# A fused mLSTM and MoE kernel: column sums in column groups, a turned branch, and attention steps moved in two chunks

## Chip, cores, metric

One core of one Trainium2 chip. The metric is the device time of one execution in microseconds (us). Runs are compared in the same state: for one core, a run that lies over 1.5% above the fastest of its kernel counts as slow and is left out of ratios. A ratio is the mean time of one kernel's fast runs over the mean of the other's fast runs of the same rounds, so it is not quite the ratio of the medians quoted beside it.

In profile lines PE is TensorE, PEld its weight loads, ACT ScalarE, DVE VectorE, POOL GpSimd and SP SyncE; a q behind a name is that engine's instruction queue. `a<-b` names an output and its inputs, and a bracket at the end of a line is the idle time before it and what ended it. PSUM is the memory that matrix products are written to; `hp` is the tile there that holds the product with w_in. The tail is the time from the start of the last VectorE output operation to the end of the span.

## The reference

Two stages, the second on the result of the first, in float32 at the outside:

```
q, k, v, o_gate: [4, 8, 768, 40]   i_gate, f_gate: [4, 8, 768]
for t in range(768):                      # per batch and head: a matrix memory C, a vector n
    C = f_stab * C + i_stab * outer(v[t], k[t]);   n = f_stab * n + i_stab * k[t]
    y[t] = sigmoid(o_gate[t]) * (C @ q[t]) / max(|n . q[t]|, 1)
x = y as [3072, 320]                      # tokens x (heads * head_dim)
g = s * relu(x @ w_in) ** 2 + b           # w_in: [320, 2048]
out = g @ w_out                           # w_out: [2048, 320]
```

The kernel uses that b adds the same row to every token: `out = s * (relu(..)**2 @ w_out) + b * colsum(w_out)`. The column sums of w_out, spread over 128 partitions and times b, are the tile `brep`.

## The kernel before

Tokens are handled in six chunks of 512. While the matrix products of chunk c run (16 steps of about 1.28 us), the attention of chunk c+1 is put between them at fixed steps by `put(chunk, step, ...)`. A general block for other gate values stands behind a branch at the end and is jumped over. Parts (cuts marked):

```python
self.psH = ctx.enter_context(tc.tile_pool(name="psH", bufs=2, space=PSUM))   # the two hp buffers
...
def load_x(self, bb, eng, names="qo"):          # 640 KB of q, then 640 KB of o_gate
    ...
    eng.dma_start(out=self.x32[nm, bb, 0], in_=src)

def relu(self, c, k, a):                        # ScalarE; frees an hp buffer
    self.nc.scalar.activation(out=r1, in_=self.hp.pop((c, k, a)), func=ACT.Relu)

def bias(self, f0, f1):                         # column sums, spread, with a matrix of ones
    ...
    for f in range(f0, f1):
        nc.tensor.matmul(ps[:], lhsT=self.ones[:], rhs=self.wo[:, f, :], start=(f == 0), stop=(f == NF - 1))
    if f1 == NF:
        nc.vector.tensor_scalar_mul(out=self.brep, in0=ps, scalar1=self.bc[:, 0:1])

def events(self):
    ...
    put(0, 15, self.bias, 0, 8)
    put(1, 0, self.vw, 2, a.copy)               # cast of v, batch 2, on ScalarE
    put(0, 15, self.kw, 2)                      # kp = k * weights, batch 2, on VectorE
    put(1, 1, self.bias, 8, NF)
    ... 2: (1, 2, 4, 6, 8, 1, 2, 6, 9, 11),     # chunk 2: q0, r0, t0, h0, y0, q1, r1, t1, h1, y1
        # q: cast q on ScalarE   r: transposing DMA on SP   t: tanh   h: ps_h   y: transposing DMA of x
    put(1, 2, self.ev_cn, 2)                    # needs v and kp of batch 2
    put(1, 3, self.load_x, 3, self.nc.sync)     # chunk 3's q and o_gate, on SP

def run(self):
    ...
    for k in range(4):
        if c > 0:
            self.mm1_rem(c, k, 0)               # 2 matmuls of 64 rows, into one hp buffer each
            self.mm1_rem(c, k, 1)
        for a in range(2):
            self.mm1(c, k, a)                   # 4 whole matmuls into hp
            self.square(*prev); self.relu(c, k, a)
            ...                                 # two steps of events, each with mm2 of chunk c-1

with tc.If(short.asked > 0, preferred_fallthrough_block=False), ExitStack() as inner:
    Full(inner, tc, short).run()
```

Of the kernel before, what the change touches and what calls it, by code (L numbers as in the profile page):

```python
# [8 lines left out]
F32 = mybir.dt.float32  # L9
# [22 lines left out]
class Short:  # L32
# [50 lines left out]
    def load_rest(self):  # L83
        nc, d = self.nc, self.d
        nc.gpsimd.dma_start(out=self.sc, in_=d["s"].partition_broadcast(P))
        nc.gpsimd.dma_start(out=self.bc, in_=d["b"].partition_broadcast(P))
        self.load_kv(2, B, nc.gpsimd)

    def load_rest2(self, eng):
        d = self.d  # L90
# [72 lines left out]
    def masks_late(self):  # L163
        nc, c = self.nc, self.const
        self.tri42 = c.tile([P, P], BF16, name="tri42")
        nc.gpsimd.memset(self.tri42, 1.0)
        nc.gpsimd.affine_select(
            out=self.tri42, in_=self.tri42, pattern=[[1, P]], base=0, channel_multiplier=-1,
            compare_op=ALU.is_ge, fill=0.0,
        )  # L170
        self.sel = c.tile([P, 3, L], BF16, name="sel")
        nc.gpsimd.tensor_copy(out=self.sel, in_=self.idb[:, 0:L].unsqueeze(1).to_broadcast([P, 3, L]))
        nc.gpsimd.memset(self.ib2[:, :, 1:2], 2.0)

    def gates(self):

# [145 lines left out]
    def ev_h(self, c, i, early=False):  # L322
        nc = self.nc
        bb, _ = self.pair(c, i)
        pool, tag = (self.psH, "hp") if early else (self.psB, "b")
        ps = pool.tile([P, 2, 512], F32, tag=tag, name="ps_h")
        qt = self.qt.pop((c, i))
        for j in range(2):
            for g in range(3):
                w = 123 if g < 2 else 82  # L330
                if c >= B and j == 0:
                    lhs, rhs = self.pm[bb][:, g, :], self.vbd[bb]
                else:
                    lhs, rhs = qt[0 : 3 * D, j, g, :], self.cn[bb]
                nc.tensor.matmul(  # L335
                    ps[:, j, g * 123 : g * 123 + w], lhsT=lhs,
                    rhs=rhs[:, g, :, :].rearrange("k a e -> k (a e)")[:, 0:w], start=True, stop=True,
                )
        hv = ps[:, :, 0 : H * (D + 1)].rearrange("p j (h e) -> p j h e", h=H)

        d1 = self.work.tile([P, 2, H], F32, tag="d1", name="d1")
        if c >= B:
            nc.vector.scalar_tensor_tensor(
                out=d1, in0=hv[:, :, :, D], scalar=-2.0,
                in1=self.ib2[:, bb * H : (bb + 1) * H, :].rearrange("p h j -> p j h"), op0=ALU.mult, op1=ALU.max,
            )
        else:
            nc.vector.tensor_scalar(  # L348
                out=d1, in0=hv[:, :, :, D], scalar1=-2.0, scalar2=2.0, op0=ALU.mult, op1=ALU.max
            )  # L350
        dd = self.work.tile([P, 2, H], F32, tag="dd", name="dd")
        nc.vector.scalar_tensor_tensor(
            out=dd, in0=hv[:, :, :, D], scalar=2.0, in1=d1, op0=ALU.mult, op1=ALU.max
        )
        rec = self.work.tile([P, 2, H], F32, tag="rec", name="rec")
        nc.vector.reciprocal(
            out=rec[:, :, :].rearrange("p j h -> p (j h)"), in_=dd[:, :, :].rearrange("p j h -> p (j h)")
        )
        fac = self.work.tile([P, 2, H, D], F32, tag="fac", bufs=2, name="fac")
        x = self.x[c, i] = self.work.tile([P, 2, DM + 64], BF16, tag="x", name="x")  # L360
        th = self.th.pop((c, i))
        for j in (slice(0, 1), slice(1, 2)) if early else (slice(0, 2),):
            nc.vector.tensor_tensor(  # L363
                out=fac[:, j, :, :], in0=hv[:, j, :, 0:D],
                in1=rec[:, j, :].unsqueeze(3).to_broadcast([P, j.stop - j.start, H, D]), op=ALU.mult,
            )
            nc.vector.scalar_tensor_tensor(  # L367
                out=x[:, j, 0:DM], in0=th[:, j, :, :].rearrange("p j h d -> p j (h d)"), scalar=1.0,
                in1=fac[:, j, :, :].rearrange("p j h d -> p j (h d)"), op0=ALU.add, op1=ALU.mult,
            )  # L370
            nc.vector.tensor_copy(out=x[:, j, DM:], in_=x[:, j, 2 * P : DM])

    def ev_x(self, c, i, js=(0, 1)):
        nc = self.nc
        x = self.x[c, i]
        ps = self.psO.tile([P, 2, 3, P], BF16, tag=self.spare, name="ps_x")
        for kts in ((0, 1), (2,)):
            for j in js:
                for kt in kts:
                    nc.tensor.transpose(ps[:, j, kt, :], x[:, j, kt * P : (kt + 1) * P], self.idb[:])  # L380
        t0 = self.pair(c, i)[1]
        nc.scalar.copy(out=self.xt[:, t0 + js[0] : t0 + js[-1] + 1, :, :], in_=ps[:, js[0] : js[-1] + 1, :, :])  # L382

# [52 lines left out]
        f = 4 * k + a  # L436
        self.nc.vector.tensor_tensor(out=self.g[c][:, f : f + 3 : 2, :], in0=r1, in1=r1, op=ALU.mult)  # L437

    def bias(self, f0, f1):
        nc = self.nc  # L440
        if f0 == 0:
            self.ps_b = self.psB.tile([P, DM], F32, tag="b", name="ps_b")
        ps = self.ps_b
        for f in range(f0, f1):
            nc.tensor.matmul(ps[:], lhsT=self.ones[:], rhs=self.wo[:, f, :], start=(f == 0), stop=(f == NF - 1))  # L445
        if f1 == NF:
            self.brep = self.keep.tile([P, DM], F32, name="brep")
            nc.vector.tensor_scalar_mul(out=self.brep, in0=ps, scalar1=self.bc[:, 0:1])

    def mm2(self, c, tb, f0, f1, pool=None):  # L450
        nc = self.nc
        if f0 == 0:
            if pool is None:
                self.o2[c, tb] = self.psO.tile([P, DM], F32, tag=f"o{tb % 2}", name="o2")
            else:
                self.o2[c, tb] = self.psH.tile([P, DM], F32, tag="hp", name="o2t")
        for f in range(f0, f1):
            nc.tensor.matmul(  # L458
                self.o2[c, tb][:], lhsT=self.g[c][:, f, tb * P : (tb + 1) * P], rhs=self.wo[:, f, :],
                start=(f == 0), stop=(f == NF - 1),  # L460
            )
        if f1 == NF:
            osb = self.work.tile([P, DM], F32, tag="osb", bufs=5, name="osb")
            nc.vector.scalar_tensor_tensor(  # L464
                out=osb, in0=self.o2.pop((c, tb)), scalar=self.sc[:, 0:1], in1=self.brep, op0=ALU.mult, op1=ALU.add
            )
            out = self.d["out"]
            if c < B:
                r0 = c * S + P
                dst = out[r0 : r0 + N, :].rearrange("(p j) n -> p j n", j=CT)[:, tb, :]  # L470
            else:
                i, j = divmod(tb, 2)
                r0 = self.pair(c, i)[0] * S + 5 * P * j
                dst = out[r0 : r0 + P, :]
            eng = nc.gpsimd if c < 3 else nc.sync
            eng.dma_start(out=dst, in_=osb)  # L476



# [46 lines left out]
    def events(self):  # L526
# [10 lines left out]
        put(0, 3, self.ev_q, 1, 0, v)  # L537
        put(0, 3, self.ev_q, 1, 1, v, True)
        put(0, 5, self.tanh, 1, 0)
        put(0, 6, self.ev_h, 1, 0)  # L540
        put(0, 6, self.square, 0, 0, 1)
        put(0, 7, self.tanh, 1, 1)
        put(0, 10, self.ev_x, 1, 0)
        put(0, 10, self.ev_h, 1, 1)
        for n in range(2, 8):
            put(0, 9 + min(n, 6), self.square, 0, n // 2, n % 2)
        put(0, 15, self.ev_x, 1, 1)
        put(0, 15, self.bias, 0, 8)
        put(1, 0, self.vw, 2, a.copy)
        put(0, 15, self.kw, 2)  # L550
        put(1, 10, self.vw, 3, a.copy)
        put(1, 1, self.bias, 8, NF)
        for c in range(2, 6):
            d = c - 1

            q0, r0, t0, h0, y0, q1, r1, t1, h1, y1 = {
                2: (1, 2, 4, 6, 8, 1, 2, 6, 9, 11),
                3: (-7, -6, 0, 1, 4, -6, -4, 2, 5, 8),
            }.get(c, (-11, -10, 0, 1, 4, -10, -9, 2, 5, 8))
            for at, step in (  # L560
# [12 lines left out]
            if c >= B:  # L573
                put(d - 1, 14, self.ev_s, c, 0)
                put(d, 3, self.ev_s, c, 1)
        put(1, 2, self.ev_cn, 2)
        put(1, 12, self.kw, 3)
        put(1, 14, self.ev_cn, 3)
        put(2, 8, self.make_tri)
        for c, b0 in ((2, 0), (3, 2)):  # L580
# [1 line left out]
            put(c, 11, self.ev_vr, b0)  # L582
            put(c, 12, self.ev_kt, b0 + 1)
            put(c, 15, self.ev_vr, b0 + 1)
        put(1, 3, self.load_x, 3, self.nc.sync)
        put(1, 14, self.load_rest2, self.nc.sync)
        put(1, 14, self.load_y, 0, self.nc.sync)
        put(2, 10, self.load_y, 2, self.nc.sync)
# [7 lines left out]
    def start(self):  # L596
# [12 lines left out]
        self.masks_late()  # L609
        for k in range(4):  # L610
            self.load_wo(k)
        self.load_x(2, nc.gpsimd)
        self.ps_w = self.psO.tile([P, 512], F32, tag="o0", name="ps_w")
        self.warm(34)
# [22 lines left out]
    def run(self):  # L637
        nc, tc = self.nc, self.tc
        with tc.manual_schedule():
# [3 lines left out]
            for c in range(6):  # L643
                for k in range(4):
# [4 lines left out]
                    elif k == 0:  # L649
# [3 lines left out]
                            self.mm1(0, 0, a, 0, N // 2)  # L653
                            self.ev_x(0, 1, (a,))
                        self.ev_cn(1)
                        self.warm(8)
                    for a in range(2):
                        if c == 0:
                            n0 = N // 2 if k == 0 else 0
# [185 lines left out]
def kernel(  # L845
# [16 lines left out]
    with ExitStack() as inner:  # L862
        short.pools(inner)
        short.run()
    with tc.If(short.asked > 0, preferred_fallthrough_block=False), ExitStack() as inner:
        Full(inner, tc, short).run()


# [28 lines left out]
```

## Time and profile before

| | before |
|---|---|
| time, median of 3 runs | 142.49 us (142.13 to 142.72) |
| span of the profiled run | 140.5 us |
| TensorE (PE) busy | 133.6 us, 95% |
| chunk 1's first whole matmuls (L423) begin | 29.67 us |
| chunk 2 begins (64-row matmuls, L411 x4) | 49.55 us |
| last VectorE output operation to end of span | 4.86 us |

### The profile page before, as it was taken

To read this page: it belongs to the slowest core of one execution; us is meant where nothing else is said; L and a number is where in the kernel's file an instruction comes from. 1 tells how busy PE (TensorE), PEld (TensorE's weight loads), DVE (VectorE), ACT (ScalarE), POOL (GpSimd) and SP (SyncE) were. 2 spreads that over 40 slices of the span, in tenths; PEclk is the share of its full clock that TensorE was granted. 3 is DMA by queue.
4 is the path that set the end of the run, shared out by engine and by line. 5 is a ranking of instruction groups with operands and counts; after the bars stand their busy time and mean duration, and the time that the engine had idled before them with its cause. 6 is when DMAs were issued, how large, how long until landed. Compare 5 with 4: busy or idle time off the path is not lost.

```text
span 140.5 us, 2582 instructions
## 1 busy us (share of the span) xinstructions
PE 133.6 (95%) x979; PEld 78.2 (56%) x979; DVE 91.5 (65%) x201; ACT 69.9 (50%) x91; POOL 26.8 (19%) x58
## 2 busy tenths in 40 slices
PE   6998999999999999999999999999999999999960
PEld 7985643446555655565565465555545545557730
DVE  6679748895499759776769956688962635335130
ACT  3273479758559545943366653383435443550000
POOL 6889399100101110011011011100000000000000
PEclk9999999999999999999999999999999999999998
DMA  3999969994899899999983471017221110011211
GB/s 41 316 217 272 283 121 122 191 314 132 176 324 178 171 200 212 210 155 148 215 127 61 103 159 47 0 47 88 66 58 47 47 51 18 34 49 49 96 51 56
DMA packets 42412, 18.45 MB, mean 131 GB/s; under 512 B 31840, under 2 KB 41376, under 8 KB 42392
## 3 DMA queue, kind: packets, MB, share of 16 engines
q1 hardware_dynamic: 36412, 10.67, 38.2%
q0 software_dynamic: 5280, 7.43, 23.8%
q10 hardware_dynamic: 700, 0.11, 0.5%
q8 instruction: 9, 0.15, 0.5%
q14 instruction: 11, 0.09, 0.2%
HBM read 13.75 MB, written 3.93 MB: 126 GB/s over the span
## 4 chain that ended last, share of the span: by engine, by line
PE 76%; DVE 0%; issue 0%
PE o L458 31%; PE hp L423 26%; PE hp L411 8%; PE o2t L458 6%; PE ps_h L335 2%; PE ps_b L445 1%; PE ps_vr L256 1%; PE ps_s L313 0%; PE ps_kt L241 0%; DVE osb L464 0%; PE ps_cn L226 0%; PE ps_fl L502 0%; PE ps_fm L509 0%; PE ps_tri L204 0%
## 5 line engine op out<-in xcount | busy, mean ns | idle before, releaser
L430 ACT ACTIVATE r<-hp 128x1024 bf16<-128x1024 f32 x48 | 49.0, 1024 | 47.6 <-PE hp L423 44.4
L458 PE MATMUL o<-wo,g 128*128 128x320 bf16 x320 | 52.7, 299 | 0.0
L423 PE MATMUL hp<-xt,wi 128*128 128x512 bf16 (+1 forms) x200 | 49.9, 372 | 0.0
L458 PEld LDWEIGHTS <-g 128*128 128x128 bf16 x384 | 36.4, 98 | 17.8
L437 DVE TENSOR_TENSOR g<-r 128x1024 bf16<-128x1024 bf16 x48 | 32.5, 685 | 9.9 <-ACT r L430 9.7
L423 PEld LDWEIGHTS <-wi 128*128 128x128 bf16 x200 | 17.1, 97 | 22.6 <-issue 9.4
L476 POOL DMA_DIRECT2D out_dram<-osb x12 | 6.5, 544 | 59.4 <-DVE osb L464 59.4
L464 DVE SCALAR_TENSOR_TENSOR osb<-o,sc,brep 128x320 f32<-128x320 f32 x20 | 10.9, 548 | 9.1 <-PE o L458 8.7
L411 PE MATMUL hp<-xt,wr 64*128 64x512 bf16 (+1 forms) x100 | 15.8, 373 | 0.4 <-ACT xt L382 0.2
L367 DVE SCALAR_TENSOR_TENSOR x<-th,fac 128x640 bf16<-128x640 f32 (+1 forms) x14 | 10.2, 730 | 1.3
L524 PE MATMUL ps_w<-ones 128*128 128x128 bf16 x106 | 9.7, 258 | 1.1 <-POOL ones L134 1.1
L363 DVE TENSOR_TENSOR fac<-ps_h,rec 128x640 f32<-128x640 f32 (+1 forms) x14 | 10.2, 728 | 0.4
L524 PEld LDWEIGHTS <-ones 128*128 128x128 bf16 x106 | 8.3, 118 | 1.1 <-POOL ones L134 1.1
L458 PE MATMUL o2t<-wo,g 128*128 128x320 bf16 x64 | 8.9, 299 | 0.0
L411 PEld LDWEIGHTS <-wr 64*128 64x128 bf16 x100 | 3.6, 94 | 8.0 <-issue 7.3
L464 DVE SCALAR_TENSOR_TENSOR osb<-o2t,sc,brep 128x320 f32<-128x320 f32 x4 | 2.2, 551 | 5.7 <-PE o2t L458 5.7
L292 ACT ACTIVATE th<-ox 128x640 f32<-128x640 f32 x8 | 5.7, 729 | 0.2 <-DMA ox<-in_o_gate_dram 0.2
L288 ACT CAST qb<-qx 128x160 bf16<-128x160 f32 (+1 forms) x11 | 4.2, 443 | 2.9 <-DMA qx<-in_q_dram 2.9
L335 PE MATMUL ps_h<-cn,qt 120*128 120x123 bf16 (+1 forms) x60 | 5.0, 212 | 0.0
L382 ACT COPY xt<-ps_x 128x384 bf16<-128x384 bf16 (+1 forms) x6 | 3.5, 584 | 3.0 <-PE ps_x L380 3.0
L335 PEld LDWEIGHTS <-qt 120*128 120x128 bf16 x60 | 3.8, 98 | 1.0 <-DVE qt L306 0.2
L348 DVE TENSOR_SCALAR d<-ps_h 128x16 f32<-128x16 f32 x8 | 1.4, 173 | 4.4 <-PE ps_h L335 4.4
(98 smaller groups left out, 87.6 us busy)
## 6 DMA issues: line engine op xcount, KB each, us to landing
out_dram<-osb POOLq DMA_DIRECT2D x12, 160.0 KB, 2.9
out_dram<-osb SPq DMA_DIRECT2D x12, 160.0 KB, 1.8
qx<-in_q_dram SPq DMA_DIRECT2D x2, 640.0 KB, 4.8
ox<-in_o_gate_dram SPq DMA_DIRECT2D x2, 640.0 KB, 6.7
qx<-in_q_dram POOLq DMA_DIRECT2D x2, 640.0 KB, 8.7
ox<-in_o_gate_dram POOLq DMA_DIRECT2D x2, 640.0 KB, 9.2
wo<-in_moe_w_out_dram POOLq DMA_DIRECT2D x4, 320.0 KB, 6.9
qy<-in_q_dram SPq DMA_DIRECT2D x8, 160.0 KB, 4.2
```

The costliest lines, as they stand in the source:

```text
L292: self.nc.scalar.activation(out=th, in_=self.src("o", c, i), func=ACT.Tanh, scale=0.5)
L335: nc.tensor.matmul(ps[:, j, g * 123 : g * 123 + w], lhsT=lhs, rhs=rhs[:, g, :, :].rearrange("k a e -> k (a e)")[:, 0:w], start=True, stop= ...
L363: nc.vector.tensor_tensor(out=fac[:, j, :, :], in0=hv[:, j, :, 0:D], in1=rec[:, j, :].unsqueeze(3).to_broadcast([P, j.stop - j.start, H, D ...
L367: nc.vector.scalar_tensor_tensor(out=x[:, j, 0:DM], in0=th[:, j, :, :].rearrange("p j h d -> p j (h d)"), scalar=1.0, in1=fac[:, j, :, :]. ...
L411: nc.tensor.matmul(hp[:, e, n0:n1], lhsT=self.wr[64 * e : 64 * e + 64, k, a * P : (a + 1) * P], rhs=self.xt[64 * e : 64 * e + 64, t0:t1, 2 ...
L423: nc.tensor.matmul(hp[:, e, n0:n1], lhsT=self.wi[:, kt, f * P : (f + 1) * P], rhs=self.xt[:, t0:t1, kt, :], start=False, stop=(kt == 1),)
L430: self.nc.scalar.activation(out=r1, in_=self.hp.pop((c, k, a)), func=ACT.Relu)
L437: self.nc.vector.tensor_tensor(out=self.g[c][:, f : f + 3 : 2, :], in0=r1, in1=r1, op=ALU.mult)
L458: nc.tensor.matmul(self.o2[c, tb][:], lhsT=self.g[c][:, f, tb * P : (tb + 1) * P], rhs=self.wo[:, f, :], start=(f == 0), stop=(f == NF - 1),)
L464: nc.vector.scalar_tensor_tensor(out=osb, in0=self.o2.pop((c, tb)), scalar=self.sc[:, 0:1], in1=self.brep, op0=ALU.mult, op1=ALU.add)
L476: eng.dma_start(out=dst, in_=osb)
L524: self.nc.tensor.matmul(self.ps_w[:, 0:P], lhsT=self.ones[:], rhs=self.ones[:], start=True, stop=True)
```

## The change

Intent: take PE work out of the bias (16 matmuls of the full array become 16 in four column groups of 32, which may run side by side, and three for the spread); shorten the start; let the branch be jumped over without a late jump; and move steps of chunks 0 and 1 to fit. `kv` of batch 2 is loaded between the parts of w_out. The core of the diff:

```diff
@@ load_rest / start
-        self.load_kv(2, B, nc.gpsimd)
             self.load_wo(k)
+            if k == 1:
+                self.load_kv(2, B, nc.gpsimd)
@@ masks_late: self.fours, zero but for rows 0, 32, 64, 96 (cut)
@@ ev_h / ev_x: chunks 0 and 1 do not copy x's last 64 columns, but transpose them twice
-            nc.vector.tensor_copy(out=x[:, j, DM:], in_=x[:, j, 2 * P : DM])
+            if c > 1:
+                nc.vector.tensor_copy(out=x[:, j, DM:], in_=x[:, j, 2 * P : DM])
+            for a in (0, 64):
+                nc.tensor.transpose(ps[a : a + 64, j, 2, :], x[:, j, 2 * P : DM], self.idb[:])
@@ bias(f0, f1) becomes
+    def colsum(self):
+        for f in range(NF):
+            j = 32 * (f % 4)
+            nc.tensor.matmul(
+                ps[j : j + 32, :], lhsT=self.ones[:, 0:32], rhs=self.wo[:, f, :], start=(f < 4), stop=(f >= NF - 4)
+            )
+        ... three bfloat16 parts ws0..2 of ps, five VectorE operations (cut)
+    def bias(self):
+        for i in range(3):
+            nc.tensor.matmul(ps[:], lhsT=self.fours[:], rhs=self.ws[i], start=(i == 0), stop=(i == 2))
+        nc.vector.tensor_scalar_mul(out=self.brep, in0=ps, scalar1=self.bc[:, 0:1])
@@ mm2: the output part becomes osb(c, tb); block (0, 0) is put out later, by an event
-        if f1 == NF:
+        if f1 == NF and (c, tb) != (0, 0):
+            self.osb(c, tb)
@@ events (squares, ev_h and ev_x of chunk 0 moved too, cut)
-        put(0, 15, self.bias, 0, 8)
-        put(0, 15, self.kw, 2)
-        put(1, 1, self.bias, 8, NF)
-        put(1, 2, self.ev_cn, 2)
+        put(1, 0, self.kw, 2)
         put(1, 0, self.vw, 2, a.copy)
+        put(1, 1, self.ev_cn, 2)
+        put(1, 3, self.colsum)
+        put(1, 6, self.bias)
+        put(1, 7, self.osb, 0, 0)
-                2: (1, 2, 4, 6, 8, 1, 2, 6, 9, 11),
+                2: (4, 5, 7, 8, 10, 4, 5, 9, 10, 12),
-        put(1, 3, self.load_x, 3, self.nc.sync)
+        put(1, 6, self.load_x, 3, self.nc.sync)
@@ run
-                        self.warm(8)
+                        self.warm(2)
-    with tc.If(short.asked > 0, preferred_fallthrough_block=False), ExitStack() as inner:
+    with tc.If(short.asked > 0, preferred_fallthrough_block=True), ExitStack() as inner:
```

More of the change, by code (lines that the diff above doesn't have):

```diff
@@ L173, in masks_late @@
         nc.gpsimd.memset(self.ib2[:, :, 1:2], 2.0)
+        self.fours = c.tile([P, P], BF16, name="fours")
+        nc.gpsimd.memset(self.fours, 0.0)
+        for j in range(0, P, 32):
+            nc.gpsimd.memset(self.fours[j : j + 1, :], 1.0)
     def gates(self):
@@ L376, in ev_x @@
         ps = self.psO.tile([P, 2, 3, P], BF16, tag=self.spare, name="ps_x")
-        for kts in ((0, 1), (2,)):
-            for j in js:
-                for kt in kts:
-                    nc.tensor.transpose(ps[:, j, kt, :], x[:, j, kt * P : (kt + 1) * P], self.idb[:])
+        for j in js:
+            for kt in range(2):
+                nc.tensor.transpose(ps[:, j, kt, :], x[:, j, kt * P : (kt + 1) * P], self.idb[:])
+            for a in (0, 64):
+                nc.tensor.transpose(ps[a : a + 64, j, 2, :], x[:, j, 2 * P : DM], self.idb[:])
         t0 = self.pair(c, i)[1]
@@ L437, in square @@
         self.nc.vector.tensor_tensor(out=self.g[c][:, f : f + 3 : 2, :], in0=r1, in1=r1, op=ALU.mult)
-    def bias(self, f0, f1):
+    def colsum(self):
         nc = self.nc
-        if f0 == 0:
-            self.ps_b = self.psB.tile([P, DM], F32, tag="b", name="ps_b")
-        ps = self.ps_b
-        for f in range(f0, f1):
-            nc.tensor.matmul(ps[:], lhsT=self.ones[:], rhs=self.wo[:, f, :], start=(f == 0), stop=(f == NF - 1))
-        if f1 == NF:
-            self.brep = self.keep.tile([P, DM], F32, name="brep")
-            nc.vector.tensor_scalar_mul(out=self.brep, in0=ps, scalar1=self.bc[:, 0:1])
+        ps = self.psB.tile([P, DM], F32, tag="b", name="ps_c")
+        for f in range(NF):
[3 more added lines that the diff above has]
+            )
+        rest = ps
+        self.ws = []
+        for i in range(3):
+            part = self.const.tile([P, DM], BF16, name=f"ws{i}")
+            nc.vector.tensor_copy(out=part, in_=rest)
+            self.ws.append(part)
+            if i < 2:
+                r = self.const.tile([P, DM], F32, name=f"wr{i}")
+                nc.vector.tensor_sub(out=r, in0=rest, in1=part)
+                rest = r
+    def bias(self):
+        nc = self.nc
+        ps = self.psB.tile([P, DM], F32, tag="b", name="ps_b")
+        for i in range(3):
+            nc.tensor.matmul(ps[:], lhsT=self.fours[:], rhs=self.ws[i], start=(i == 0), stop=(i == 2))
+        self.brep = self.keep.tile([P, DM], F32, name="brep")
+        nc.vector.tensor_scalar_mul(out=self.brep, in0=ps, scalar1=self.bc[:, 0:1])
     def mm2(self, c, tb, f0, f1, pool=None):
@@ L461, in mm2, with osb @@
             )
-        if f1 == NF:
-            osb = self.work.tile([P, DM], F32, tag="osb", bufs=5, name="osb")
-            nc.vector.scalar_tensor_tensor(
-                out=osb, in0=self.o2.pop((c, tb)), scalar=self.sc[:, 0:1], in1=self.brep, op0=ALU.mult, op1=ALU.add
-            )
-            out = self.d["out"]
-            if c < B:
-                r0 = c * S + P
-                dst = out[r0 : r0 + N, :].rearrange("(p j) n -> p j n", j=CT)[:, tb, :]
-            else:
-                i, j = divmod(tb, 2)
-                r0 = self.pair(c, i)[0] * S + 5 * P * j
-                dst = out[r0 : r0 + P, :]
-            eng = nc.gpsimd if c < 3 else nc.sync
-            eng.dma_start(out=dst, in_=osb)
+        if f1 == NF and (c, tb) != (0, 0):
+            self.osb(c, tb)
+    def osb(self, c, tb):
+        nc = self.nc
+        osb = self.work.tile([P, DM], F32, tag="osb", bufs=5, name="osb")
+        nc.vector.scalar_tensor_tensor(
+            out=osb, in0=self.o2.pop((c, tb)), scalar=self.sc[:, 0:1], in1=self.brep, op0=ALU.mult, op1=ALU.add
+        )
+        out = self.d["out"]
+        if c < B:
+            r0 = c * S + P
+            dst = out[r0 : r0 + N, :].rearrange("(p j) n -> p j n", j=CT)[:, tb, :]
+        else:
+            i, j = divmod(tb, 2)
+            r0 = self.pair(c, i)[0] * S + 5 * P * j
+            dst = out[r0 : r0 + P, :]
+        eng = nc.gpsimd if c < 3 else nc.sync
+        eng.dma_start(out=dst, in_=osb)
     def flag_a(self):
@@ L539, in events @@
         put(0, 5, self.tanh, 1, 0)
-        put(0, 6, self.ev_h, 1, 0)
-        put(0, 6, self.square, 0, 0, 1)
+        put(0, 5, self.ev_h, 1, 0)
         put(0, 7, self.tanh, 1, 1)
-        put(0, 10, self.ev_x, 1, 0)
-        put(0, 10, self.ev_h, 1, 1)
+        put(0, 8, self.ev_x, 1, 0)
+        put(0, 8, self.ev_h, 1, 1)
+        put(0, 11, self.square, 0, 0, 1)
         for n in range(2, 8):
             put(0, 9 + min(n, 6), self.square, 0, n // 2, n % 2)
-        put(0, 15, self.ev_x, 1, 1)
-        put(0, 15, self.bias, 0, 8)
+        put(0, 12, self.ev_x, 1, 1)
+        put(1, 0, self.kw, 2)
         put(1, 0, self.vw, 2, a.copy)
-        put(0, 15, self.kw, 2)
-        put(1, 10, self.vw, 3, a.copy)
-        put(1, 1, self.bias, 8, NF)
+        put(1, 1, self.ev_cn, 2)
+        put(1, 3, self.colsum)
+        put(1, 6, self.bias)
+        put(1, 7, self.osb, 0, 0)
+        put(1, 11, self.vw, 3, a.copy)
         for c in range(2, 6):
```

## The prediction

> **What bounds the kernel now.** I read the page first (busy shares, slices), then the chain of work that ended last in order of time, then the timeline of each engine from 0 to 50 us, then the branch's own instructions.
>
> ```profile
> span 140.5 us, 2582 instructions
> PE 133.6 (95%) x979; PEld 78.2 (56%) x979; DVE 91.5 (65%) x201; ACT 69.9 (50%) x91; POOL 26.8 (19%) x58
> ```
>
> TensorE is busy 95% of the span, so only three things can move the end: work taken out of PE's stream, waits put into or taken out of it, and the tail after it. The chain shows where the stream is solid.
>
> ```profile
> 29.09 0.04 issue
> 29.13 0.61 PE hp L411 x4
> 29.74 0.97 PE hp L423 x4
> 30.71 0.41 PE o L458 x3
> 31.11 1.09 PE ps_b L445 x8
> ...
> 49.62 0.54 PE hp L411 x4
> ```
>
> Columns: start, length, what. From 29.1 us (chunk 1 begins) to 135.7 PE goes from one instruction to the next. 49.62 is where chunk 2 begins. Half of the bias (8 matmuls, 1.09 us) is in this solid stretch. The other half fills time before chunk 1:
>
> ```profile
> 27.65 1.25 PE L445 MATMUL ps_b<-wo,ones 128*128 128x320 bf16 x8
> 29.13 0.61 PE L411 MATMUL hp<-xt,wr 64*128 64x512 bf16 x4 [0.23 <-ACT xt L382]
> ```
>
> After those 8 matmuls PE still waits 0.23 us for the transposed x of chunk 1. So this half costs next to nothing today. Next, the lines of ScalarE and of the DMA queue of SP in chunk 1, which the moved steps touch:
>
> ```profile
> 30.80 1.02 ACT L430 ACTIVATE r<-hp 128x1024 bf16<-128x1024 f32 x1 [1.72 <-issue]
> 31.71 0.45 ACT L220 CAST v<-v 42x320 bf16<-42x320 f32 x1
> 32.85 1.54 ACT L288 CAST qb<-qx 128x480 bf16<-128x480 f32 x4 [0.69 <-DMA qx<-in_q_dram]
> 33.69 2.66 SPq L388 DMA_TRANSPOSE qt<-qb  x2
> 36.46 0.53 SPq L103 DMA_DIRECT2D qx<-in_q_dram  x1
> 42.52 0.81 ACT L288 CAST qb<-qx 128x480 bf16<-128x480 f32 x2
> 43.59 1.02 ACT L430 ACTIVATE r<-hp 128x1024 bf16<-128x1024 f32 x1 [0.26 <-PE hp L423]
> ```
>
> The reader is to see an order: the casts of chunk 2's q release the two transposing DMAs, behind these SP issues the load of chunk 3's q (36.46, landed 4.9 us later, at 41.4), and that load releases the cast at 42.52, behind which stands a relu that frees a PSUM buffer. Today the load lands 1.1 us before it is asked for. Last, the branch:
>
> ```profile
> L865 PEldq COMPARE_BRANCH  x2: 95/1910/3725, 133.1 to 135.8; - x2
> L865 DVEq COMPARE_BRANCH  x2: 51/53/55, 135.7 to 136.4; - x2
> ```
>
> PE passes the comparison at 133.1, then takes the jump over the general block at 135.8, and it takes 3.7 us: the program's last barrier starts at 139.6, 3.4 us after the last VectorE result.
>
> **What the skill says.** (1) The Trainium skill, "Runtime: NRT & Kernel Launch", section "Instruction fetch mechanics": a taken branch whose target lies outside the two fetched pages costs a DMA fetch before going on. The trace agrees: a 16 KB instruction packet runs from 136.80 to 138.13 inside that jump, and the last output's final packets[...] run only after it (138.13 to 139.03). (2) "TensorEngine Tiling (Array Packing)", section "Key Properties": tiles of different columns work in parallel, and a change of tiling mode drains the array. The trace has row tiles only: four 64-row matmuls of 512 columns take 0.54 us (L411 x4), against 0.86 for four whole ones (L423 x4). As two pairs at 0.22 would be 0.43, about 0.1 us is left for the change of mode and back. (3) "TensorE: Matmul & The Clock Gate", section "Part 3: Packing small matmuls — row/col tiling" gives 2.38x for three column tiles; no run here shows column tiles yet.
>
> **The change part by part.** Chunks are counted from 0; each has 16 steps of about 1.28 us.
>
> *Bias.* Removed: 16 x 0.136 = 2.18 us of PE, of which 1.09 is in the solid stretch. Added in chunk 1: 16 column sums in four column groups, an estimate of 2.18/3.1 = 0.7 us from the skill's factors (ideal 0.55), and the spread, 3 x 0.136 = 0.41. Sum in the solid stretch: 0.7 + 0.41 - 1.09, about **0**, and 0.15 with the mode changes. VectorE gets five more operations on 128x320 (about 2.4 us) in chunk 1; they end 1 us before the spread wants them.
>
> *Start and chunk 0.* The four 64-column copies of x go: x to copy to next operation took 0.53 + 0.09 us, x straight to the next about 0.41, so 0.2 us each, 0.8 at the end of VectorE's start chain (kp 14.62 to 13.8). Each x gets one matmul more and mode changes (0.1 us). Warm-ups fall from 8 to 2. PE's second half of the first matmuls moves from 15.91 to about 15.1. Then q of batch 1 binds, landed at 15.92: its transposes go from 17.33 only to 17.1. From 17.55 I step PE with 1.29 us for each (k, a), 0.4 for ps_h, 0.65 for eight transposes: last matmuls of chunk 0 end at 27.4. But no filler is left at the border: the second pair of chunk 1 needs the buffer of the last relu, 27.5 + 1.02. So chunk 1's L423 starts at about 28.9 instead of 29.67: **-0.8 us**.
>
> *Chunk 1, ev_cn one step earlier.* It now stands 0.41 us behind the first matmuls, but reads v, cast on ScalarE behind the relu of these matmuls: 0.08 + 0.91 + 0.45 + 0.1 = 1.5 us after they end (lines at 30.80 and 31.71). PE waits **+1.1 us** there.
>
> *Chunk 1, attention of chunk 2 three steps later.* Casts at step 4, and SP's load of chunk 3's q stays behind their transposes, but its cast stays at step 9. Let T be the end of PE's matmuls of k=1, a=0 (36.72 before). Relu to T+1.0; from the start of the casts to the landing of q took 41.4 - 32.85 = 8.5: T+9.5; cast 0.8, relu 1.0: the buffer is free at T+11.4. PE wants it at T + 0.81 + 0.86 + 0.41 + 1.36 + 0.54 + 0.97 + 0.3 + 0.81 + 0.86 + 0.3 + 1.36 + 0.27 = T+8.9. That is a wait of 2.5 us; with less traffic beside it the load may be quicker, so **+2.1**. The two ps_h now 2 us apart also wait for each other's PSUM buffer, 0.15.
>
> *Branch.* The long jump is now taken by the comparison itself, on PE 2.6 us earlier, beside its last matmuls; the last output loses its collision. VectorE's jump moves only from 136.37 to 135.7, and its fetch then ends the tail: **-0.7 us** (1.1 if only the output counts).
>
> Sum: 0.15 - 0.8 + 1.1 + 2.1 + 0.15 - 0.7 = **+2.0**, so 144.5 us by the steps. From there on every chunk is as before.
>
> **Rivals.** *A: the tuning is right and chunk 1 has no new wait.* Then 0.15 - 0.8 - 0.7, 141.1 us. For it: the steps were plainly moved together, as for a later landing of q (the loads of k and v now stand between w_out's). Against it: the cast order on ScalarE and the load order on SP are fixed by the program, and the slack was 1.1 us. *B: startup gives more.* If PE, not relu, sets the border of chunk 0, and only half of the chunk 1 waits come, 142 us. Against: the buffer count is two. *C: column groups do not overlap, or w_out lands late.* The column sums need all of w_out, whose last part landed at 30.5 and now comes behind k and v; I reckon 31.7 against a need at 33.6. If both go wrong, +1.5 us more, 146 us.
>
> **Range and chances.** The two waits in chunk 1 rest on program order and I hold them at two in three; A and B share most of the rest. Weighted: 0.65 x 144.5 + 0.3 x 141.6 + 0.05 x 146 = 143.7. I predict 143.7 us, range 141.0 to 145.4. The limits of 2% are 139.6 and 145.3: faster 0.05, same 0.82, slower 0.13.
>
> **What would show it.** Right: ScalarE's cast of chunk 3's q waits some 2.5 us for its DMA, and PE's L-row pair behind it waits for a relu; ps_cn of batch 2 waits about 1 us for the cast of v; PE waits about 0.9 us for a relu between chunks 0 and 1; column sums 0.6 to 0.9 us for 16; chunk 2 begins near 52 instead of 49.62; the tail after the last VectorE operation is 0.7 us shorter. Wrong: chunk 2 begins before 49.6, or those casts wait for nothing; then A holds.

## More of the kernel before

One more stretch is used later as a measure, the end of chunk 1 in PE's timeline before the change (start, length, engine, line, operation, tiles, shapes, count):

```profile
46.25 0.98 PE L458 MATMUL o<-wo,g 128*128 128x320 bf16 x6
47.07 1.03 PE L423 MATMUL hp<-xt,wi 128*128 128x512 bf16 x4
...
49.55 0.60 PE L411 MATMUL hp<-xt,wr 64*128 64x512 bf16 x4
```

No line has a bracket with idle time: PE waits for nothing, and six matmuls of 320 columns take 0.98 us at full clock.

## The result, and the profile after

| | before | after |
|---|---|---|
| time, median | 142.31 us (142.03 to 142.72) | 148.91 us (148.30 to 148.99, 4 runs) |
| ratio, 95% interval | | 1.0452 (1.0412 to 1.0492): slower |
| span of the profiled run | 140.5 us | 147.1 us |
| first whole matmuls of chunk 1 | 29.67 | 29.26 |
| chunk 2 begins | 49.55 | 56.66 |
| last VectorE output operation to the end | 4.86 | 4.33 |

The times before are those taken beside the changed kernel. Line numbers move: L411, L423, L430, L458 and L288 of before are L417, L429, L436, L481 and L292 of after. All ten experiments gave correct results.

From the start of chunk 2 to the last VectorE output operation both kernels take 86.1 us. So the whole difference of 6.6 us of span is +7.11 up to the start of chunk 2 and -0.53 in the tail. PE's timeline after shows where the 7.11 are:

```profile
28.93 0.39 PE L417 MATMUL hp<-xt,wr 64*128 64x512 bf16 x2 [0.79 <-ACT r L436]
...
31.80 0.33 PE L230 MATMUL ps_cn<-v,kp 128*120 128x123 bf16 x3 [1.10 <-ACT v L224]
...
34.01 0.73 PE L451 MATMUL ps_c<-wo,ones 128*32 128x320 bf16 x16
...
44.35 0.47 PE L339 MATMUL ps_h<-cn,qt 120*128 120x123 bf16 x6 [0.38 <-DMA qt<-qb]
...
50.53 0.43 PE L417 MATMUL hp<-xt,wr 64*128 64x512 bf16 x2 [4.03 <-ACT r L436]
50.89 1.89 PE L429 MATMUL hp<-xt,wi 128*128 128x512 bf16 x4
52.57 1.77 PE L481 MATMUL o<-wo,g 128*128 128x320 bf16 x6
54.17 1.03 PE L429 MATMUL hp<-xt,wi 128*128 128x512 bf16 x4
...
56.66 0.61 PE L417 MATMUL hp<-xt,wr 64*128 64x512 bf16 x4
```

The reader is to see two things. The brackets give idle time and what ended it: 0.79, 1.10, 0.38 and 4.03 us. And right behind the longest wait the same work takes longer: 1.89 us for four whole matmuls and 1.77 for six of 320 columns, against 1.03 and 0.98 before. The windows of this kernel (PE, PEld, DVE, ACT and POOL busy with counts, granted TensorE clock, DMA share, which this view can print above 1, GB/s) name the reason, a clock of 0.50:

```profile
47.00:50.80 3.80, 0.27 (x2) 0.09 (x1) 1.83 (x5) 2.06 (x4) 0.54 (x1) 0.99 1.52 191
50.80:54.20 3.40, 3.40 (x13) 1.52 (x12) 1.13 (x3) 1.77 (x4) 0.00 (x0) 0.50 0.95 229
54.20:58.00 3.80, 3.80 (x26) 1.97 (x25) 2.06 (x4) 1.02 (x1) 0.39 (x1) 1.00 0.86 163
```

The relu that ends the 4.03 us stands on ScalarE behind a cast that waits for a load. ScalarE's timeline after:

```profile
38.03 1.53 ACT L292 CAST qb<-qx 128x480 bf16<-128x480 f32 x4
...
48.74 0.82 ACT L292 CAST qb<-qx 128x480 bf16<-128x480 f32 x2 [5.07 <-DMA qx<-in_q_dram]
49.46 1.01 ACT L436 ACTIVATE r<-hp 128x1024 bf16<-128x1024 f32 x1
```

The load was issued by SP at 41.65 and landed 7.07 us later, at 48.72; before, the same load took 4.9. The DMA view of 40 to 50 us:

```profile
qx<-in_q_dram SPq DMA_DIRECT2D x1, 640.0 KB, 7.1
```

SP's and GpSimd's timelines after show what went into the queues around it:

```profile
38.87 2.67 SPq L394 DMA_TRANSPOSE qt<-qb  x2
41.65 0.66 SPq L102 DMA_DIRECT2D qx<-in_q_dram  x1
```

```profile
40.59 0.57 POOL L503 DMA_DIRECT2D out_dram<-osb  x1 [14.73 <-DVE osb L491]
41.36 0.55 POOL L503 DMA_DIRECT2D out_dram<-osb  x1 [0.20 <-issue]
```

Two output blocks of 160 KB leave back to back just ahead of the load. Before, they left at 35.88 and 42.18. The later bias holds block (0, 0) back, as no output can be formed without `brep`.

### The profile page after: what moved, and what is told of

The parts are those of the page before. It is cut to its first block, busy times and chain, and to the rows that moved or that the text cites. A ratio compares the mean times of both kernels' runs of the same rounds, so it can differ in the third digit from the quotient of the medians.

```text
span 147.1 us, 2593 instructions
## 1 busy us (share of the span) xinstructions
PE 135.1 (92%) x984; PEld 77.8 (53%) x984; DVE 92.6 (63%) x200; ACT 69.9 (48%) x91; POOL 28.0 (19%) x63
## 3 DMA queue, kind: packets, MB, share of 16 engines
HBM read 13.75 MB, written 3.93 MB: 120 GB/s over the span
## 4 chain that ended last, share of the span: by engine, by line
PE 65%; DMA 5%; ACT 3%; DVE 2%; issue 1%; SPq 0%; ACTq 0%
PE o L481 26%; PE hp L429 22%; PE hp L417 6%; PE o2t L481 6%; DMA qx<-in_q_dram 5%; ACT r L436 1%; PE ps_h L339 1%; ACT qb L292 1%; DVE ws L458 1%; PE ps_vr L260 1%; DVE wr L462 1%; PE ps_s L317 0%; PE ps_c L451 0%; PE ps_kt L245 0%; ACT th L296 0%
## 5 line engine op out<-in xcount | busy, mean ns | idle before, releaser
L436 ACT ACTIVATE r<-hp 128x1024 bf16<-128x1024 f32 x48 | 49.0, 1023 | 50.7 <-PE hp L429 46.4
L481 PE MATMUL o<-wo,g 128*128 128x320 bf16 x320 | 53.5, 302 | 0.0
L429 PE MATMUL hp<-xt,wi 128*128 128x512 bf16 (+1 forms) x200 | 50.8, 377 | 0.0
L481 PEld LDWEIGHTS <-g 128*128 128x128 bf16 x384 | 36.6, 99 | 18.5 <-issue 0.8
L429 PEld LDWEIGHTS <-wi 128*128 128x128 bf16 x200 | 17.3, 98 | 22.8 <-issue 9.7
L417 PE MATMUL hp<-xt,wr 64*128 64x512 bf16 (+1 forms) x100 | 16.0, 374 | 5.0 <-ACT r L436 4.8
L417 PEld LDWEIGHTS <-wr 64*128 64x128 bf16 x100 | 3.7, 94 | 12.7 <-issue 11.6
L481 PE MATMUL o2t<-wo,g 128*128 128x320 bf16 x64 | 8.9, 299 | 0.0
L292 ACT CAST qb<-qx 128x160 bf16<-128x160 f32 (+1 forms) x11 | 4.2, 443 | 7.3 <-DMA qx<-in_q_dram 7.3
L235 DVE TENSOR_TENSOR cn<-ps_cn,bdm 120x369 bf16<-120x369 f32 x4 | 2.2, 544 | 3.5 <-PE ps_cn L230 3.5
```

The costliest lines, as they stand in the source:

```text
L417: nc.tensor.matmul(hp[:, e, n0:n1], lhsT=self.wr[64 * e : 64 * e + 64, k, a * P : (a + 1) * P], rhs=self.xt[64 * e : 64 * e + 64, t0:t1, 2 ...
L429: nc.tensor.matmul(hp[:, e, n0:n1], lhsT=self.wi[:, kt, f * P : (f + 1) * P], rhs=self.xt[:, t0:t1, kt, :], start=False, stop=(kt == 1),)
L481: nc.tensor.matmul(self.o2[c, tb][:], lhsT=self.g[c][:, f, tb * P : (tb + 1) * P], rhs=self.wo[:, f, :], start=(f == 0), stop=(f == NF - 1),)
```

## The experiments

Ten kernels ran, in three calls; runs of one call share the runs of the kernel before (medians 142.5, 142.47 and 142.66 us). "Chunk 2 begins" is read from PE's timeline as above.

| run | made from | time, median | ratio to before, 95% | span | chunk 2 begins |
|---|---|---|---|---|---|
| a_x3pool | after | 144.93 | 1.0150 (1.0111 to 1.0189) | 143.3 | 51.74 |
| a_warm | after | 148.55 | 1.0395 (1.0345 to 1.0444) | 146.8 | 55.02 |
| a_outlate | after | 147.02 | 1.0310 (1.0269 to 1.0350) | 144.9 | 54.44 |
| a_vwearly | after | 148.17 | 1.0377 (1.0327 to 1.0426) | 145.8 | 55.41 |
| b_branch | before | 141.70 | 0.9948 (0.9915 to 0.9981) | 139.4 | 49.04 |
| b_colsum | before | 143.44 | 1.0074 (1.0039 to 1.0109) | 141.6 | 49.93 |
| b_moves | before | 147.33 | 1.0235 (1.0148 to 1.0321), unclear | 145.5 | 54.52 |
| a_x3_vw | after | 142.31 | 1.0019 (0.9964 to 1.0074) | 140.6 | 50.45 |
| best1 | after | 142.75 | 1.0008 (0.9974 to 1.0043) | 140.9 | 50.74 |
| best2 | after | 140.92 | 0.9859 (0.9817 to 0.9900) | 140.2 | 48.37 |

Counted as slow and left out of the ratios are one run each of a_vwearly (150.81), b_branch (143.47) and best1 (144.25), and two of b_moves. Positions read from one trace carry the scatter of the start phase: of the four kernels whose chunk 0 starts as before, the first whole matmuls of chunk 1 begin at 29.67 (before), 29.37 (b_branch), 29.37 (b_colsum) and 30.29 us (b_moves).

**The theory:** of the two waits in chunk 1, the load of chunk 3's q is the large one; it costs the wait itself and a stretch of slow clock behind it. **The rivals:** the slow clock has another cause; the load is late by its own place in the queue and not by the outputs; the column sums or the branch cost time of their own.

### The load of chunk 3's q out of the way (a_x3pool)

```diff
-        put(1, 6, self.load_x, 3, self.nc.sync)
+        put(1, 0, self.load_x, 3, self.nc.gpsimd)
```

> The changed kernel with the load of chunk 3's q and o issued by GpSimd behind that of chunk 2, instead of by SP behind the transposes of chunk 2's q. Theory 1 (the late load blocks ScalarE in order, the relu behind it holds TensorE, and the idle TensorE falls to half clock): the 4.03 us wait of the matmul pair at 46.1 and the slow stretch behind it (1.55 us) both go, chunk 2 begins at about 51.0 instead of 56.66, 143.3 us. Theory 2 (the three-step shift of chunk 2's attention is itself too late: transposes of q and x, VectorE's extra five operations): the load was only the last to arrive, another wait of 2 us or more takes its place, 145.5 us or more.

The long wait and the slow clock are both gone; chunk 2 begins 4.92 us earlier. PE's timeline of this run:

```profile
47.62 0.98 PE L481 MATMUL o<-wo,g 128*128 128x320 bf16 x6
48.43 1.03 PE L429 MATMUL hp<-xt,wi 128*128 128x512 bf16 x4
49.78 0.38 PE L230 MATMUL ps_cn<-v,kp 128*120 128x123 bf16 x3 [0.32 <-DVE kp L216]
```

So the place of this one load carries most of the loss. The time fell by less (4.0 us) because the tail grew by 1.1 us in this run, so that 144.93 lies between the two times expected, and the trace decides; the tail is taken up below.

### Work in the wait (a_warm)

```diff
                         self.mm1_rem(c, k, 0)
+                        if (c, k) == (1, 3):
+                            ps = self.psB.tile([P, 512], F32, tag="b", name="ps_fill")
+                            for _ in range(56):
+                                nc.tensor.matmul(ps[:, 0:P], lhsT=self.ones[:], rhs=self.ones[:], start=True, stop=True)
                         self.mm1_rem(c, k, 1)
```

> The changed kernel with 56 filler matmuls (128x128, about 3.3 us) put into the 4 us wait. The wait stays, so the load is as late as before; only TensorE's idleness goes. If the slow matmuls after the wait come from the idleness, they run at full speed and the time falls by 1.5 us to 147.4. If they come from something else (traffic, the buffer), it stays at 148.9.

```profile
47.11 3.30 PE L681 MATMUL ps_fill<-ones 128*128 128x128 bf16 x56 [0.62 <-DVE fac L367]
50.52 0.39 PE L417 MATMUL hp<-xt,wr 64*128 64x512 bf16 x2
50.85 1.04 PE L429 MATMUL hp<-xt,wi 128*128 128x512 bf16 x4
```

The second pair starts at 50.52, as without fillers (50.53), so the relu is as late as before; but the matmuls behind it run at full clock, and chunk 2 begins 1.64 us earlier. That is the price of the slow clock by itself, and the idle PE is its cause. The time by itself, 148.55, is nearer to what the rival said (148.9) than to the 147.4 expected, because the tail of this run is 1.37 us longer.

### The two outputs away from the load (a_outlate)

```diff
+        if (c, tb) in ((0, 0), (0, 1)):
+            self.held.append((dst, osb))
+            return
         eng.dma_start(out=dst, in_=osb)
+        put(1, 12, self.late)        # issues what is held, on GpSimd
```

> The changed kernel with the DMAs of the first two output blocks issued at step 12 of chunk 1 instead of directly after their computation at steps 7. Theory: these 2 x 160 KB, now back to back, stood ahead of chunk 3's q in the rings and made its load 7.07 us instead of 4.92. Then it lands about 2 us earlier (46.7), the wait is 2.0 us instead of 4.0, the slow clock shrinks or goes, and the time is 145.5 to 146.9. If the transposes or the bandwidth of q's own small packets made it long, it stays within 0.5 us of 148.9.

The load, issued at 41.60, landed after 4.9 us instead of 7.07. The line of the DMA view, and PE's timeline:

```profile
qx<-in_q_dram SPq DMA_DIRECT2D x1, 640.0 KB, 4.9
```

```profile
48.31 0.49 PE L418 MATMUL hp<-xt,wr 64*128 64x512 bf16 x2 [2.20 <-ACT r L437]
48.73 1.89 PE L430 MATMUL hp<-xt,wi 128*128 128x512 bf16 x4
```

The wait is 2.20 us, near the 2.1 of the prediction. The two outputs beside the load are the other 1.8. The slow clock comes even behind the shorter wait, and so the time, 147.02, is just above the range expected. The two other traces with both outputs ahead of the load on SP repeat the long load: 7.06 us in a_warm and 6.93 in a_vwearly.

### The two moves alone, in the kernel before (b_moves)

```diff
-                2: (1, 2, 4, 6, 8, 1, 2, 6, 9, 11),
+                2: (4, 5, 7, 8, 10, 4, 5, 9, 10, 12),
-        put(1, 3, self.load_x, 3, self.nc.sync)
+        put(1, 6, self.load_x, 3, self.nc.sync)
```

> The kernel before with two moves alone: attention of chunk 2 three steps later (casts of q at step 4) and the load of chunk 3's q at step 6 of chunk 1, still on SP behind the transposes of chunk 2's q; bias, start and branch as before. Theory: these two alone make the late wait. PE waits at the second pair of 64-row matmuls of chunk 1's k=3, and a half-clock window follows; the first output goes out early here, so that only one of two outputs runs beside the load: a wait of about 3 us rather than 4.0, plus 1.5 for the clock, 146.5 to 147.5 us. Rival: the moves do harm only together with column sums and the deferred outputs: no wait over 1 us, below 144.

```profile
48.34 0.39 PE L411 MATMUL hp<-xt,wr 64*128 64x512 bf16 x2 [2.13 <-ACT r L430]
48.66 1.24 PE L423 MATMUL hp<-xt,wi 128*128 128x512 bf16 x4
49.70 1.80 PE L458 MATMUL o<-wo,g 128*128 128x320 bf16 x6
51.30 1.76 PE L423 MATMUL hp<-xt,wi 128*128 128x512 bf16 x4
```

The wait is 2.13 us, not the 3 that I expected: with one output (issued at 41.05) beside it, the load takes 4.8 us, no more than with none. Only with a second output close behind the first did it take 7.07; why two cost so much more than one, no run here settles. The slow clock falls on three groups: 1.24 + 1.80 + 1.76 against 1.03 + 0.98 + 1.03 at full clock, 1.76 us. Chunk 1 of this run began 0.62 us later than in the profile before, by the start phase, which varies between runs. The times spread over 145.2 to 147.64 us, two of the four runs count as slow, the profiled one among them, so no conclusion here rests on the median; the wait and its order are read from the trace. The spread has a reason: the run of 145.2 us has a mean granted clock of 0.995, the others 0.983 to 0.986. One slow stretch of 3.41 us at half clock would by itself leave about 0.988 in that run (an estimate, 1 - 1.71/143.2), so it went without one. It is 2.0 to 2.4 us faster than the others, about the price of the slow stretch (1.76); its wait seems to have stayed, but it left no trace. A wait of this length then does not bring the slow clock every time.

### The cast of v back in its place (a_vwearly)

```diff
-        put(1, 0, self.vw, 2, a.copy)
+        put(0, 15, self.vw, 2, a.copy)
```

> The changed kernel with the cast of v for batch 2 placed one step earlier on ScalarE, ahead of the first relu of chunk 1 instead of behind it. The wait of 1.10 us of ps_cn goes, and as the late load's wait hangs on the step before it by a fixed distance, the whole 1.1 us reaches the end: 147.8 us. Rival: the later wait is set by absolute times of DMA and swallows it: 148.9 us.

The wait of ps_cn is gone and chunk 2 begins 1.25 us earlier, for a wait printed as 1.10. (Idle time is counted from the modelled end of the matmul before, so each printed wait is some 0.14 us too small.) The time fell by 0.7 us of the 1.1 expected.

### The column sums alone (b_colsum)

The kernel before with `colsum` and `bias` as in the change, at steps 3 and 5 of chunk 1, and nothing else.

> The kernel before with the bias alone changed: column sums in four column groups, split in three bfloat16 parts, spread by three matmuls; all moves, loads and the branch as before. Theory: no gain, 142.4 us within 0.3, as half of the old bias only filled time ahead of chunk 1, which waits for transposed x anyhow, and 1.09 in the solid stretch is replaced by about 0.7 and 0.41. Rival: PE's work falls by 2.18 - 1.1 = 1.1 us and the time with it: 141.4 us.

PE's timeline of this run, where the group of eight bias matmuls ahead of chunk 1 is gone:

```profile
28.83 0.61 PE L416 MATMUL hp<-xt,wr 64*128 64x512 bf16 x4 [1.32 <-ACT xt L387]
...
35.32 0.39 PE L416 MATMUL hp<-xt,wr 64*128 64x512 bf16 x2 [0.60 <-ACT r L435]
```

The 1.25 us of matmuls that stood there became a wait of 1.32 for the same transposed x. So half of the bias was filler, as the prediction says. What comes after, 0.73 for the column sums and 0.57 for the spread as groups, takes the place of the other half, and PE then waits 0.60 for a relu that stands behind the casts of q. This part by itself gains nothing; the 143.44 us are 1 us above what I expected, and the ratio says a loss of 0.7%. Of the 1.07 us that the span of this trace is longer, 0.38 lie ahead of chunk 2. The other 0.69 are tail (5.55 against 4.86), although the branch is as before.

### The branch alone (b_branch)

```diff
-    with tc.If(short.asked > 0, preferred_fallthrough_block=False), ExitStack() as inner:
+    with tc.If(short.asked > 0, preferred_fallthrough_block=True), ExitStack() as inner:
```

> The kernel before with the branch alone turned round (general block directly behind the branch). Theory of the prediction: the jump is taken by the comparison, beside the last matmuls, the tail behind the start of the last VectorE output operation falls from 4.86 us to about 4.3: about 142.0 us. Rival, from the trace of a_x3pool: the jump starts a second instruction fetch some 1.6 to 2.0 us behind that operation; if it starts before the packets of the last output, these run late and the tail is about 5.4 to 5.7 us: about 143.2. The trace tells which.

It gains 0.5%. In its trace 0.62 us of the 1.1 are the shorter tail; chunk 2 also begins 0.51 us earlier, which is scatter, as nothing was changed ahead of it. The branch in the profile after, to be read against the same rows of before in the prediction:

```profile
L895 PEldq COMPARE_BRANCH  x1: 3835/3835/3835, 140.2 to 140.2; - x1
L895 DVEq COMPARE_BRANCH  x1: 72/72/72, 142.8 to 142.8; - x1
```

One comparison on each engine instead of two; PE's takes 3.8 us, but starts 2.6 us ahead of the last VectorE operation, beside PE's last matmuls. Tail: 4.24 us here, 4.86 before.

The gain is not safe. In all traces with the turned branch, a second 16 KB instruction fetch follows the first. In a_x3pool, a_warm and best2 it starts 1.62 to 1.69 us after the start of the last VectorE output operation, the last output's packets end at 3.84 to 3.93, and the tail is 5.4 to 5.7 us. In after, a_outlate, a_vwearly, b_branch, a_x3_vw and best1 it starts at 1.91 to 2.04, the packets are done by 2.2 to 2.4, and the tail is 4.0 to 4.3. Nine traces in two groups without overlap make the collision likely; no experiment moved the fetch by itself. The run of 143.47 us, left out as slow, has an undiminished clock (0.998) and may be such a long tail; it left no trace. The tail of the old branch varies too: it is 4.86 (before), 4.86 (b_moves) and 5.55 us (b_colsum, where the fetch starts at 1.91 instead of 1.12).

### The two waits mended together (a_x3_vw)

The edits of a_x3pool and a_vwearly in one kernel.

> The kernel after with two of its moves mended: the load of chunk 3's q goes to GpSimd's queue at the start of chunk 1, and the cast of v of batch 2 goes back ahead of the relu (end of chunk 0). Theory: both waits are gone, the gains add up: chunk 2 begins near 50.5 (51.74 with the load alone, less 1.25 of the cast alone), about 143.7 us, half a microsecond less or more by the tail. Rival: the cast only moves the wait to the relu behind it, so that the two do not add up: 144.9 as with the load alone.

Chunk 2 begins at 50.45; 51.74 - 1.25 would be 50.49. The two waits add up, as expected. The time is 1.4 us below the 143.7 expected, as the tail is 3.99 us, against 5.41 in the run that I had reckoned from. What is left of the change is as fast as the kernel before (1.0019) and no faster. It still waits 0.79 for the relu at the border of the chunks, 0.38 for qt and 0.35 for kp.

### Two versions with more mended (best1, best2)

best1 also moves chunk 2's attention one step earlier and, at the border, puts the second pair's 64-row matmuls behind the first pair's whole ones:

```diff
-                2: (4, 5, 7, 8, 10, 4, 5, 9, 10, 12),
+                2: (3, 4, 6, 7, 9, 3, 4, 8, 9, 11),
                         self.mm1_rem(c, k, 0)
-                        self.mm1_rem(c, k, 1)
+                        if (c, k) != (1, 0):
+                            self.mm1_rem(c, k, 1)
...
+                            if (c, k, a) == (1, 0, 1):
+                                self.mm1_rem(c, k, a)
                             self.mm1(c, k, a)
```

> The kernel after with the two mended moves, the attention of chunk 2 one step earlier (3 and 4 instead of 4 and 5), and at the border of chunk 0 and 1 the second pair's 64-row matmuls put behind the first pair's whole ones, so that the wait for the relu has work in front of it. Theory: all that remains of the change is what helps (column sums, shorter start, jump), so chunk 2 begins near 48.6 to 49.4 and the time is 140.7 to 142.0 us, by the tail. Rival: the border wait stays (buffer count two), 142.5 us or more.

```profile
30.44 0.38 PE L230 MATMUL ps_cn<-v,kp 128*120 128x123 bf16 x3 [0.76 <-DVE kp L216]
...
40.09 0.47 PE L339 MATMUL ps_h<-cn,qt 120*128 120x123 bf16 x6 [1.19 <-DMA qt<-qb]
```

The border wait is gone, but two others took its place: kp stands behind seven squares on VectorE, and the transposes, issued at 34.35 while the early loads of chunk 3 (landed at 37.3 and 39.5) still run, are done 5.7 us later. My expectation failed. best2 mends just these two, with the edits of best1 but for the load:

```diff
-        put(1, 0, self.kw, 2)
+        put(0, 14, self.kw, 2)
-        put(1, 6, self.load_x, 3, self.nc.sync)
+        put(1, 5, self.load_x, 3, self.nc.sync)
```

> The kernel after, mended by what its own waits and those of best1 showed: cast of v and attention weights of k for batch 2 in chunk 0 (step 15 and 14), 64-row matmuls of the second pair behind the first pair's whole ones at the border, attention of chunk 2 at steps 3 and 4, and the load of chunk 3's q on SP straight behind the transposes (step 5), where it no longer slows them. Theory: the waits of best1 for kp (0.76) and for qt (1.19) are gone, chunk 2 begins near 48.8, 140.6 to 141.3 us with a tail near 4.2, below the kernel before and the branch alone (141.7). Rival: the transposes stay 5.5 us long or the load lands late again, one wait of over 1 us remains: 142 or more.

```profile
29.35 0.33 PE L230 MATMUL ps_cn<-v,kp 128*120 128x123 bf16 x3
...
37.73 0.46 PE L339 MATMUL ps_h<-cn,qt 120*128 120x123 bf16 x6
...
48.37 0.61 PE L417 MATMUL hp<-xt,wr 64*128 64x512 bf16 x4
```

No bracket is left between chunks 0 and 2, and chunk 2 begins at 48.37. The median is 140.92 us, ratio 0.9859 (0.9817 to 0.9900): 1.4% faster than the kernel before, within the 2% that count as the same, and 8 us below the kernel after, which ran in another call. The load is again on SP; issued at 36.59, it is in time. Its profiled run is the slowest of its six (142.03 us), with the long tail of 5.68; the other five have spans of 138.7 to 139.5, which fits a tail without the collision, but they left no trace.

## Why the prediction was wrong

Ledger up to the start of chunk 2, predicted against measured, in us:

| term of the prediction | predicted | measured | by |
|---|---|---|---|
| bias | +0.15 | about 0 (0.69 + 0.41 against 1.09 on the chain) | trace |
| start and chunk 0 | -0.8 | -0.41 (29.26 against 29.67), within the scatter of the start | trace |
| ev_cn one step earlier | +1.1 | +1.25 | a_vwearly |
| late load of chunk 3's q | +2.1 | +4.17 (4.03 printed, 0.14 uncounted) | trace; 2.20 in a_outlate, 2.13 in b_moves |
| slow clock behind that wait | none | +1.64 | a_warm |
| the two ps_h | +0.15 | +0.52 (0.38 + 0.14) | trace |
| sum | +2.7 | +7.17; the traces differ by 7.11 | |
| tail | -0.7 | -0.53 | trace |

**Right.** Both new waits were named with their engine, tile and releaser, and so was the border wait (predicted 0.9, measured 0.79). The bias gives nothing: b_colsum shows that half of it was filler. The jump runs beside PE's last matmuls: b_branch, -0.62 in the tail.

**The step that failed** is the term "attention of chunk 2 three steps later", by its size. Its mechanism held: casts late, transposes ahead of the load, cast of chunk 3's q behind the load, relu behind the cast. Three things in it were mis-sized:

1. The time from the start of the casts to the landing of q. The prediction took over 8.5 us from the kernel before and added that "with less traffic beside it the load may be quicker". It was 48.72 - 38.03 = 10.7. The traffic was more: the deferred bias, a part of the same change, moved two output blocks to just ahead of the load. b_moves, which has the moves without the deferred bias, gives 2.13; a_outlate takes the outputs away and gives 2.20. In both the time from the casts to the landing is again 8.4 to 8.5 us. That these waits match the +2.1 so closely is in part luck: with the uncounted 0.14 they are 2.27 and 2.34, nearer to the 2.5 of the steps, and the load was not quicker (4.8 and 4.9 us), so the 0.4 taken off had no ground. I had looked at the bias for PE and VectorE only and not asked when the outputs that wait for it would leave.
2. The clock. A wait was counted as its own length. a_warm shows 1.64 us more behind it. The profile before could not show this, as PE has no such gap there; but the Trainium skill, "TensorE: Matmul & The Clock Gate", section "Part 1: The HAM clock gate", says that an idle PE falls to half clock and that the windows are 3.4 us long. The trace agrees with the size: clock 0.50 from 50.8 to 54.2. I had cited another part of that page and did not put this one beside a predicted gap of over 2 us; read literally, its condition would have cleared such a gap (see the last section).
3. The two ps_h: 0.38 printed instead of 0.15, for the same crowded queues; it is gone in a_outlate.

The start also gave less than predicted in this trace, 0.41 instead of 0.8. VectorE's part came as forecast (kp from 14.62 to 13.87), but the last relu of chunk 0 began at 27.86 instead of 27.5. How much of the rest is scatter of the start stays open. And the weighting hid the working: the steps gave 144.5, rival A (no new wait) pulled it to 143.7, and on the other side stood only rival C with one part in twenty, for another reason; that the predicted wait itself might be longer had no weight. The range ended at 145.4 for this reason.

**Rivals.** A is refuted by b_moves, in which the two moves alone make the wait. B fails: a relu did set the border (0.79 us of wait), and the waits of chunk 1 came in full. C is refuted: the column groups overlap, 16 in 0.69 us on the chain against 2.18, and the last part of w_out landed at 31.97 for a use at 34.01.

**Open.** Why two outputs slow the load by 2.2 us and one by nothing; and whether the second instruction fetch causes the long tail, which nine traces suggest and no run isolates; also why one run of b_moves seems to have had no slow clock.

## What to carry to other kernels

When a change defers a value, follow everything that waits for it out to the DMA queues, and lay these transfers beside the other moved ones: here the moves without the deferred outputs made a wait of about the size counted (2.13 and 2.20 us), and with them one of twice that (4.03). Price a new TensorE wait of 2 us or more with a possible stretch at half clock behind it. And when a change gathers five moves, run the parts alone: two single-line edits took back 6.2 us of PE's way to chunk 2 here, and the rest, re-timed, was 1.4% ahead of the kernel before.

## What the Trainium skill lacked or had wrong

- "TensorE: Matmul & The Clock Gate", Part 1, gives at least one idle window of about 3.4 us as the condition of half clock. Here 2.20 us of idle PE (a_outlate) and 2.13 (b_moves, the profiled run) were followed by it, at full length: 1.89 us instead of 1.04 for four matmuls in a_outlate, and 3.41 us at 0.50 in all four traces that have it, from 0.2 to 1.1 us after PE went on. One run of b_moves (clock 0.995, no trace) seems to have gone without. Waits of 1.32 (b_colsum) and below were not followed by it. Where the limit lies between 1.3 and 2.1, no run here shows.
- The same page, Part 3, has three column tiles at 2.38x. Four column groups of 32 with all 128 rows in use took 0.69 us on the chain for 16 matmuls of 320 columns against 2.18 for whole ones, 3.2x. With the way into the mode and back it is about 0.76, 2.9x: the stretch from 33.24 to 35.45 less 1.45 for its ten other matmuls. The page has no measured figure for four column tiles.
- "Runtime: NRT & Kernel Launch", "Instruction fetch mechanics", says that a taken branch can cost a fetch and that pages are fetched ahead; it gives no time for either. Here, with the turned branch, a second 16 KB fetch began 1.62 to 2.04 us after the start of the last VectorE output operation in nine traces. The page also does not say that output packets beside it may end 1.5 us later (3.84 to 3.93 instead of 2.2 to 2.4).
- No page has a figure for what small outputs cost a load in another queue: a load of 640 KB took 7.07 us with two outputs of 160 KB issued just ahead of it, 4.8 and 4.9 with one, and 4.9 with none.
